# Moving the last transposes between two pairs of output tiles, and the final adds to GpSimd, in an attention and gated-MLP kernel

## The chip, the cores and the metric

The kernel runs on one core of one Trainium2 chip. The metric is the device time of one execution in microseconds (us). All runs quoted here are fast, with a mean granted TensorE clock of 0.999 or 1.0. The profile is of one execution, and its span is about 2 us shorter than that execution's device time. In the code, `ps_r` and `ps_acc` are tiles in PSUM, the memory that the matmuls write; the other tiles named here are in SBUF, the core's main on-chip memory. In the profile PE is TensorE, PEld its weight loads, DVE VectorE, ACT ScalarE, POOL GpSimd and SPq the DMA queue of SyncE. The differences of this case are below 0.1% of the time; so every experiment was timed in five rounds, beside runs of the kernel before on the same chip.

## The reference, cut to what matters

```python
xn = layernorm(x)                                   # x: 2048 x 512
q = (xn @ wq) split into 32 heads of 128            # k_cache, v_cache: 32 x 2048 x 128
p = softmax(q @ k_cache.T * 128**-0.5)
s = (p @ v_cache, heads side by side) @ wo          # 2048 x 512
g = silu(((relu(xn @ W_gate)) * (xn @ W_up)) @ W_down)
out = x + s * g
```

The output has 16 tiles of 128 rows, numbered 0 to 15. The product with `wo` is summed over groups of four heads. The first seven groups are already in `x_sb` (times `g`) when the last group is finished, so the "final add" of a tile is `x_sb += s_last * g`.

## The kernel before

TensorE is the limit of the whole kernel. Attention is a software pipeline: score matmuls, exponentials on ScalarE, probability-times-V matmuls. The final tiles 0 to 7 are produced inside that main loop. At its end the last block of 512 rows is normalised in two halves, and eight output tiles remain. Tiles 8 to 11 do not need the last block: they are the two "filler pairs" that keep TensorE busy while VectorE normalises it. Tiles 12 to 15 need it, transposed by TensorE and copied by ScalarE.

```python
def flush_last_transposes():
    s = ring_acquire()                        # one of three pairs of PSUM banks
    for k, (hh, Q, ob, bank, tok) in enumerate(pending_last):
        tp_ps = ps_r[:, 2 * s + k, :].bitcast(BF16)
        _wait(pe, tok)                        # VectorE has normalised this half
        # ... two pe.transpose of 128x128 from Onorm ...
        _wait(act, ptok)
        last_ot[bank] = sem_otc.sig(act.copy(OT_store[...], tp_ps[:, 0:256]))
    ring_tok[s] = list(last_ot.values())

def emit_final_tile(n, bank):
    # ... waits; four matmuls of 128x512 into ps_r[:, bank, 0:D] ...
    otok = sem_op.sig(ins)
    fb = fin_cnt[0] % NFT                     # NFT temporaries
    fin_cnt[0] += 1
    _wait(dve, otok)
    _wait(dve, fin_free[fb])
    mtok = sem_opa.sig(
        dve.tensor_tensor(fin_tmp[fb][:], ps_r[:, bank, 0:D], g_sb[:, n, :], ALU.mult))
    _wait(dve, mtok)
    if n == 0:
        _wait(dve, base_done[NT - 1])
    ftok = sem_opa.sig(
        dve.tensor_tensor(x_sb[:, n, :], x_sb[:, n, :], fin_tmp[fb][:], ALU.add))
    fin_free[fb] = ftok
    if Q == QB - 1 or j % 2 == 1:             # tiles 12 to 15: one store each
        n0 = n if Q == QB - 1 else n - 1
        _wait(sp, ftok)
        sem_out.sig(sp.dma_start(out_t[:, n0:n + 1, :], x_sb[:, n0:n + 1, :]))
    return mtok                               # frees the PSUM bank

# ... main loop ...
for n in range(NT - 8, NT - 4, 2):            # filler pairs (8, 9) and (10, 11)
    emit_M([(emit_final_tile, n), (emit_final_tile, n + 1)])
flush_last_transposes()
for n in range(NT - 4, NT, 2):                # (12, 13) and (14, 15)
    emit_M([(emit_final_tile, n), (emit_final_tile, n + 1)])
```

In the profile the multiply is line L767, the add L772, the output matmuls L759, the transposes L694, their copies L699, the half-tile normalisation L673 and L676, the store L777.

The softmax here doesn't subtract the row's maximum and nothing guards it: scores larger than these inputs give would overflow.

Of the kernel before, what the change touches and what calls it, by code (L numbers as in the profile page):

```python
# [5 lines left out]
BF16 = mybir.dt.bfloat16  # L6
F32 = mybir.dt.float32
ALU = mybir.AluOpType
# [21 lines left out]
def _wait(eng, tok):  # L30
    if tok is None:
        return
    sem, val = tok
    if val <= 0:
        return
    eng.wait_ge(sem.h, val)
# [15 lines left out]
def bass_recurrent_scan__mha_block_cached__glu_gated_reglu__prompt_kernel(  # L52
# [10 lines left out]
    out: bass.AP,  # L63
):
    _, S, D = A_x.shape
    _, H, Sk, Dh = A_k_cache.shape
    F = B_W_gate.shape[1]
    assert Dh == 128
# [4 lines left out]
    NT = S // 128  # L73
# [27 lines left out]
    dve = nc.vector  # L101
    sp = nc.sync
    pool = nc.gpsimd

    with ExitStack() as es:
        _cnt = [0]

        def S_(shape, dt, name):
            _cnt[0] += 1
            return es.enter_context(nc.sbuf_tensor(f"{name}_{_cnt[0]}", shape, dt))  # L110
# [4 lines left out]
        def newsem(unit=1):  # L115
            _cnt[0] += 1
            return _Sem(es.enter_context(nc.semaphore(f"sem{_cnt[0]}")), unit)
# [5 lines left out]
        x_sb = S_([128, NT, D], BF16, "x_sb")  # L123
# [53 lines left out]
        sem_xp = newsem()  # L177
# [5 lines left out]
        sem_opa = newsem()  # L183
# [14 lines left out]
        with nc.Block() as block:  # L198

            @block.tensor  # L200
            def _(_pe_eng):
# [91 lines left out]
                def wo_tok(g):  # L293
                    return (sem_wo[g % 2], 16 * (g // 2 + 1))
# [8 lines left out]
                def ring_acquire():  # L303
                    s = ring_cnt[0] % NSLOT
                    ring_cnt[0] += 1
                    _wait_all(pe, ring_tok[s])
                    ring_tok[s] = []
                    return s
# [222 lines left out]
                rz_sb = S_([128, 4, 1], F32, "rz_sb")  # L531
                Onorm = [S_([128, 4, Dh], BF16, "Onorm") for _ in range(NON)]
                OT_store = [S_([128, G, S], BF16, "OT_store") for _ in range(2)]
                fin_tmp = [S_([128, D], BF16, "fin_tmp") for _ in range(2)]

                qt_ready = {}
                qp_done_tok = {}
# [9 lines left out]
                def emit_M(items):  # L547
                    s = ring_acquire()
                    toks = [fn(*args, 2 * s + k) for k, (fn, *args) in enumerate(items)]
                    ring_tok[s] = toks  # L550
# [47 lines left out]
                base_done = {}  # L598
# [87 lines left out]
                def flush_last_transposes():  # L686
                    s = ring_acquire()
                    for k, (hh, Q, ob, bank, tok) in enumerate(pending_last):
                        tp_ps = ps_r[:, 2 * s + k, :].bitcast(BF16)
                        _wait(pe, tok)  # L690
                        ins = None
                        for jj in range(2):
                            j = 2 * bank + jj
                            ins = pe.transpose(tp_ps[:, jj * 128:(jj + 1) * 128], Onorm[ob][:, j, :], ident[:])  # L694
                        ptok = sem_ptr.sig(ins)
                        _wait(act, ptok)
                        c0 = Q * NQ + bank * 256
                        last_ot[bank] = sem_otc.sig(
                            act.copy(OT_store[(NG - 1) % 2][:, hh, c0:c0 + 256], tp_ps[:, 0:256])  # L699
                        )  # L700
                    ring_tok[s] = list(last_ot.values())
# [47 lines left out]
                def emit_final_tile(n, bank):  # L749
                    Q, j = divmod(n, 4)  # L750
                    if n == 0:
                        _wait(pe, wo_tok(gL))
                    if j == 0:
                        _wait(pe, (sem_tl[Q], sem_tl[Q].n))
                    if Q == QB - 1:
                        _wait(pe, last_ot[j // 2])
                    ins = None
                    for hh in range(G):
                        ins = pe.matmul(ps_r[:, bank, 0:D], OT_store[gL % 2][:, hh, n * 128:(n + 1) * 128],  # L759
                                        Wo_sb[gL % 2][:, hh, :], start=(hh == 0), stop=(hh == G - 1))  # L760
                    otok = sem_op.sig(ins)
                    fb = fin_cnt[0] % NFT
                    fin_cnt[0] += 1
                    _wait(dve, otok)
                    _wait(dve, fin_free[fb])
                    mtok = sem_opa.sig(
                        dve.tensor_tensor(fin_tmp[fb][:], ps_r[:, bank, 0:D], g_sb[:, n, :], ALU.mult))  # L767
                    _wait(dve, mtok)
                    if n == 0:
                        _wait(dve, base_done[NT - 1])  # L770
                    ftok = sem_opa.sig(
                        dve.tensor_tensor(x_sb[:, n, :], x_sb[:, n, :], fin_tmp[fb][:], ALU.add))  # L772
                    fin_free[fb] = ftok
                    if Q == QB - 1 or j % 2 == 1:
                        n0 = n if Q == QB - 1 else n - 1
                        _wait(sp, ftok)
                        sem_out.sig(sp.dma_start(out_t[:, n0:n + 1, :], x_sb[:, n0:n + 1, :]))  # L777
                    return mtok
# [16 lines left out]
                for Q in range(QB - 2):  # L795
                    for j in range(4):
                        plan.setdefault((LB + 2 + Q, 4 * (j // 2)), []).append((emit_final_tile, 4 * Q + j))
# [31 lines left out]
                assert not plan  # L829
                for n in range(NT - 8, NT - 4, 2):  # L830
                    emit_M([(emit_final_tile, n), (emit_final_tile, n + 1)])
                flush_last_transposes()
                for n in range(NT - 4, NT, 2):
                    emit_M([(emit_final_tile, n), (emit_final_tile, n + 1)])
                sp.wait_ge(sem_out.h, sem_out.n)
# [28 lines left out]
```

## Time and profile before

| | before |
|---|---|
| device time, median (six runs in all) | 1288.03 us (1287.91 to 1288.51) |
| span of the profiled run | 1285.8 us |
| TensorE busy | 99% of the span |
| VectorE, ScalarE, GpSimd busy | 30%, 78%, 1% |
| VectorE, pair of multiply and add, start to start, in the tail | 1.06 us |
| TensorE, four matmuls of one output tile | 0.87 us (in the chain view eight take 1.73 us) |
| last store's issue to the end of the span | 2.0 us |

Busy shares of a 1286 us span say nothing about its last 12 us. This is part 4 of the page of the kernel before, the chain of work that ended last:

```profile
PE 99%; DVE 1%; issue 0%; DMA 0%; ACT 0%
```

TensorE carries 99% of the chain, and VectorE (DVE) only 1%, but that 1% is the tail. The next lines are from the timeline of the kernel before, VectorE alone, tail only. The columns are start (us), duration (us), engine, line, operation, output and inputs, count, and in brackets the idle time before it and what ended it.

```profile
1274.13 0.17 DVE L673 RECIPROCAL rz_sb<-ps_acc 128x2 f32<-128x2 f32 x1 [0.35 <-PE ps_acc L722]
...
1275.21 0.68 DVE L767 TENSOR_TENSOR fin_tmp<-ps_r,g_sb 128x512 bf16<-128x512 f32 x1
1275.93 0.42 DVE L772 TENSOR_TENSOR x_sb<-x_sb,fin_tmp 128x512 bf16<-128x512 bf16 x1
1276.27 0.68 DVE L767 TENSOR_TENSOR fin_tmp<-ps_r,g_sb 128x512 bf16<-128x512 f32 x1
...
1282.64 0.68 DVE L767 TENSOR_TENSOR fin_tmp<-ps_r,g_sb 128x512 bf16<-128x512 f32 x1
1283.36 0.43 DVE L772 TENSOR_TENSOR x_sb<-x_sb,fin_tmp 128x512 bf16<-128x512 bf16 x1
```

There are no brackets behind the multiplies: VectorE hardly idles (it is busy for 5.90 us of the 6.11 us from 1276.20 to 1282.31). Its pairs follow each other every 1.06 us (1275.21, 1276.27), while TensorE delivers a tile every 0.87 us. So VectorE falls behind and the tail is its time: eight pairs, ending at 1283.79. The same stretch of the timeline shows TensorE and the copies that it waits for; the last row, from the timeline of SyncE, is the last store:

```profile
1277.50 0.39 PE L694 MATMUL ps_r<-ident,Onorm 128*128 128x128 bf16 x4
1277.81 0.65 ACT L699 COPY OT_store<-ps_r 128x256 bf16<-128x256 bf16 x2 [5.76 <-PE ps_r L694]
...
1278.33 3.61 PE L759 MATMUL ps_r<-Wo_sb,OT_store 128*128 128x512 bf16 x16 [0.44 <-ACT OT_store L699]
...
1283.81 0.33 SPq L777 DMA_DIRECT2D out_dram<-x_sb  x1
```

TensorE idles 0.44 us for ScalarE's copies, and still ends at 1281.94, almost 2 us before VectorE.

### The profile page before, as it was taken

How to read it: one execution, taken by the hardware profiler on the slowest of the kernel's cores; microseconds unless marked ns; L12 is line 12 of the kernel's file. 1: busy time of each engine (PE TensorE's matmuls, PEld its weight loads, DVE VectorE, ACT ScalarE, POOL GpSimd, SP SyncE). 2: the span in 40 equal slices, each digit the busy share in tenths (PEclk: the TensorE clock that was granted, in tenths of full speed). 3: DMA queues.
4: the chain of work that ended last, by engine and by line, in shares of the span. 5: the costliest groups of instructions: out<-in, count | busy, mean ns of one | idle time of the engine just before them, and what ended most of it. 6: DMA issues, size and time to landing. Idle time of an engine off the chain costs nothing.

```text
span 1285.8 us, 26847 instructions
## 1 busy us (share of the span) xinstructions
PE 1279.2 (99%) x11995; PEld 834.8 (65%) x11995; DVE 380.0 (30%) x682; ACT 1001.4 (78%) x1109; POOL 10.0 (1%) x21
## 2 busy tenths in 40 slices
PE   9999999999999999999999999999999999999998
PEld 4444476666666666666666666666666666666665
DVE  6333311112222222222222222222222222234456
ACT  3322399998888888888888888888888888888884
POOL 2000000000000000000000000000000000000000
PEclk9999999999999999999999999999999999999999
DMA  9500123232222332232322322332223321233302
GB/s 266 111 1 1 21 36 67 57 54 40 36 51 50 71 54 50 54 71 51 54 46 37 60 47 53 55 67 55 54 51 71 55 34 38 50 67 55 50 14 74
DMA packets 238801, 71.60 MB, mean 56 GB/s; under 512 B 225632, under 2 KB 238688, under 8 KB 238688
## 3 DMA queue, kind: packets, MB, share of 16 engines
q1 hardware_dynamic: 238400, 69.63, 27.8%
q8 instruction: 96, 1.57, 0.5%
q10 hardware_dynamic: 288, 0.26, 0.1%
q14 instruction: 17, 0.14, 0.0%
HBM read 32.77 MB, written 2.10 MB: 27 GB/s over the span
## 4 chain that ended last, share of the span: by engine, by line
PE 99%; DVE 1%; issue 0%; DMA 0%; ACT 0%
PE ps_acc L722 36%; PE ps_r L625 34%; PE ps_r L558 9%; PE ps_r L579 8%; PE ps_acc L504 4%; PE ps_r L485 4%; PE ps_r L481 4%; PE ps_r L759 1%; DVE fin_tmp L767 0%; PE ps_r L407 0%; DMA x_sb<-in_A_x_dram 0%; DVE stats L315 0%; ACT xnT L359 0%; PE ps_acc L353 0%; DVE x_sb L772 0%
## 5 line engine op out<-in xcount | busy, mean ns | idle before, releaser
L635 ACT ACTIVATE PT<-ps_r 128x1024 bf16<-128x1024 f32 x1024 | 952.5, 1054 | 167.7 <-PE ps_r L625 167.7
L722 PEld LDWEIGHTS ps_acc<-V_sb,PT 128*128 128x128 bf16 x8192 | 621.1, 98 | 241.7 <-ACT PT L635 3.5
L722 PE MATMUL ps_acc<-V_sb,PT 128*128 128x129 bf16 x8192 | 776.5, 220 | 0.0
L625 PE MATMUL ps_r<-QT_sb,KT_sb 128*128 128x512 bf16 x2048 | 754.1, 379 | 0.0
L652 DVE RECIPROCAL rz_sb<-ps_acc 128x4 f32<-128x4 f32 x127 | 23.3, 183 | 729.6 <-PE ps_acc L722 729.6
L625 PEld LDWEIGHTS ps_r<-QT_sb,KT_sb 128*128 128x128 bf16 x2048 | 195.0, 98 | 1.1 <-DVE QT_sb L569 0.4
L558 PE MATMUL ps_r<-xnT,Wq_sb 128*128 128x512 bf16 x512 | 130.9, 379 | 0.0
L579 PE MATMUL ps_r<-Wo_sb,OT_store 128*128 128x512 bf16 x448 | 114.6, 379 | 0.0
L569 DVE CAST QT_sb<-ps_r 128x512 bf16<-128x512 f32 x128 | 88.5, 692 | 48.1 <-PE ps_r L558 48.1
L558 PEld LDWEIGHTS ps_r<-xnT,Wq_sb 128*128 128x128 bf16 x512 | 49.9, 97 | 60.7 <-ACT PT L635 27.1
L655 DVE TENSOR_TENSOR Onorm<-ps_acc,rz_sb 128x512 bf16<-128x512 f32 x127 | 87.8, 691 | 4.4
L579 PEld LDWEIGHTS ps_r<-Wo_sb,OT_store 128*128 128x128 bf16 x448 | 43.8, 98 | 52.9 <-ACT PT L635 0.2
L448 ACT ACTIVATE gr_sb<-ps_r 128x512 bf16<-128x512 f32 x56 | 33.3, 596 | 51.5 <-PE ps_r L481 49.9
L592 DVE TENSOR_TENSOR s_acc<-s_acc,ps_r 128x512 f32<-128x512 f32 x96 | 66.0, 687 | 17.3 <-PE ps_r L579 17.3
L485 PE MATMUL ps_r<-xnT,Wu_sb 128*128 128x512 bf16 x212 | 54.4, 379 | 0.0
L481 PE MATMUL ps_r<-xnT,Wg_sb 128*128 128x512 bf16 x212 | 54.4, 379 | 0.0
L454 DVE TENSOR_TENSOR hT<-gr_sb,ps_r 128x512 bf16<-128x512 bf16 x56 | 38.4, 686 | 46.3 <-PE ps_r L485 42.0
L504 PE MATMUL ps_acc<-Wd_sb,hT 128*128 128x512 bf16 x224 | 49.0, 379 | 0.0
L510 ACT ACTIVATE sig_sb<-ps_acc 128x512 f32<-128x512 f32 x16 | 9.6, 597 | 38.8 <-PE ps_acc L504 38.8
L504 PEld LDWEIGHTS ps_acc<-Wd_sb,hT 128*128 128x128 bf16 x224 | 21.9, 98 | 26.4
L485 PEld LDWEIGHTS ps_r<-xnT,Wu_sb 128*128 128x128 bf16 x212 | 20.7, 98 | 25.0
L481 PEld LDWEIGHTS ps_r<-xnT,Wg_sb 128*128 128x128 bf16 x212 | 20.8, 98 | 24.8
(42 smaller groups left out, 138.7 us busy)
## 6 DMA issues: line engine op xcount, KB each, us to landing
V_sb<-in_A_v_cache_dram SPq DMA_DIRECT2D x32, 512.0 KB, 4.5
Wq_sb<-in_A_wq_dram SPq DMA_DIRECT2D x32, 128.0 KB, 2.4
Wo_sb<-in_A_wo_dram SPq DMA_DIRECT2D x8, 512.0 KB, 3.9
OT_store<-Onorm SPq DMA_TRANSPOSE x127, 2.4
Wd_sb<-in_B_W_down_dram SPq DMA_DIRECT2D x1, 1792.0 KB, 13.6
x_sb<-in_A_x_dram SPq DMA_DIRECT2D x3, 512.0 KB, 10.1
out_dram<-x_sb SPq DMA_DIRECT2D x6, 256.0 KB, 2.2
Wg_sb<-in_B_W_gate_dram SPq DMA_DIRECT2D x1, 768.0 KB, 9.8
```

Of the source, the lines that this page charges most:

```text
L454: dve.tensor_tensor(hT[par][:, fc, :], gr_sb[gk][:], ps_r[:, gb + 1, :], ALU.mult)
L481: ins = pe.matmul(ps_r[:, gb, :], Wg_sb[:, c, fs], xnT[:, c, qs], start=(c == 0), stop=(c == DC - 1))
L485: ins = pe.matmul(ps_r[:, gb + 1, :], Wu_sb[:, c, fs], xnT[:, c, qs], start=(c == 0), stop=(c == DC - 1))
L504: ins = pe.matmul(ps_acc[:, jb, 0:D], hT[par][:, fc, j * 128:(j + 1) * 128], Wd_sb[:, fc, :], start=(fc == 0), stop=(fc == FC - 1))
L558: ins = pe.matmul(ps_r[:, bank, :], Wq_sb[b][:, c, :], xnT[:, c, qs], start=(c == 0), stop=(c == DC - 1))
L569: etok = sem_qpe.sig(dve.tensor_copy(QT_sb[b][:, qs], ps_r[:, bank, :]))
L579: ins = pe.matmul(ps_r[:, bank, 0:D], OT_store[g % 2][:, hh, n * 128:(n + 1) * 128], Wo_sb[g % 2][:, hh, :], start=(hh == 0), stop=(hh == ...
L592: dve.tensor_tensor(s_acc[:, n, :], s_acc[:, n, :], ps_r[:, bank, 0:D], ALU.add)
L625: ins = pe.matmul(ps_r[:, 2 * s + tt, :], KT_sb[h % 2][:, t * 128:(t + 1) * 128], QT_sb[h % 2][:, qs], start=True, stop=True)
L635: act.activation(PT[pb][:], ps_r[:, 2 * s:2 * s + 2, :], ACTF.Exp, scale=scale)
L655: dve.tensor_tensor(Onorm[ob][:], o_ap, rz_sb[:].to_broadcast([128, 4, Dh]), ALU.mult))
L722: ins = pe.matmul(o_ap, PT[pb][:, tt, j * 128:(j + 1) * 128], V_sb[vb][:, t, 0:VW], start=(t == 0 and j % 2 == 0), stop=(t == KT - 1 and j ...
```

## The change

The intent is to hide TensorE's wait for the copies behind tiles 10 and 11, and to take the adds off VectorE, which lags in the tail. GpSimd is idle there. The last tile's add stays on VectorE. There are four temporaries in place of two, so that multiplies don't wait for GpSimd. This is the whole diff; unchanged lines are mostly left out:

```diff
-                fin_tmp = [S_([128, D], BF16, "fin_tmp") for _ in range(2)]
+                fin_tmp = [S_([128, D], BF16, "fin_tmp") for _ in range(4)]
@@ emit_final_tile
-                    _wait(dve, mtok)
+                    eng, sem = (dve, sem_opa) if n == NT - 1 else (pool, sem_xp)
+                    _wait(eng, mtok)
                     if n == 0:
-                        _wait(dve, base_done[NT - 1])
-                    ftok = sem_opa.sig(
-                        dve.tensor_tensor(x_sb[:, n, :], x_sb[:, n, :], fin_tmp[fb][:], ALU.add))
+                        _wait(eng, base_done[NT - 1])
+                    ftok = sem.sig(
+                        eng.tensor_tensor(x_sb[:, n, :], x_sb[:, n, :], fin_tmp[fb][:], ALU.add))
@@ end
                 for n in range(NT - 8, NT - 4, 2):
                     emit_M([(emit_final_tile, n), (emit_final_tile, n + 1)])
-                flush_last_transposes()
+                    if n == NT - 8:
+                        flush_last_transposes()
```

## The prediction

> **What bounds the kernel now.** The page gives TensorE 99% busy of a 1285.8 us span at full clock, and the chain of waits is 99% TensorE. The change touches only the last ~12 us, where the chain is different. There it leaves TensorE at 1274.1 us (end of the last probability-times-V matmuls) and runs on VectorE to the end: after the last two normalisations come eight pairs of a multiply (128x512 out of PSUM, 0.68 us) and an add (128x512 bf16, 0.43 us). Starts of multiplies in the timeline: 1275.21, 1276.27, ... 1282.64, a pair every 1.06 us. TensorE needs only about 0.865 us per output tile (16 matmuls in 3.6 us) and ends at 1281.9 us, so VectorE is the limit of the tail by then: last add ends at 1283.79 us, the last store takes the remaining 2.0 us.
>
> **What the change does.**
> 1. Transposes after the first filler pair: TensorE waited 0.6 us in all (waits view: 0.59 us of weight load, 0.44 us of matmul, overlapping) for ScalarE's two copies of 0.32 us. Now tiles 10 and 11 (1.7 us of matmuls) hide them. The norm results are ready at 1275.3, before TensorE reaches the transposes (about 1275.8). TensorE ends about 0.4 us earlier, at 1281.5. This was not on the critical chain, since VectorE lagged.
> 2. VectorE loses seven of the eight tail adds. Alone it would follow TensorE: last multiply about 1281.6 to 1282.3, last add to 1282.75, 1.0 us earlier than before.
> 3. GpSimd takes seven adds in the tail (tiles 8 to 14), on two SBUF inputs. No such add is in the trace. A one-input GpSimd pass over 128x512 bf16 starts every 0.75 us here. The Trainium skill, "GPSIMD Engine Reference", section "Performance versus the Vector engine", states about 1.8 cycles per element [...] (768 ns for 512, which this trace shows: 768 ns mean) and about 2.6 for a two-input add. My estimate from both: 2.6/1.8 x 0.768 = 1.11 us, with dispatch 1.1 to 1.2. That is slower than VectorE's whole pair (1.06 us). First add starts at about 1276.0; seven take 7.8 to 8.4 us and end at 1283.8 to 1284.4.
> 4. The last add stays on VectorE with two SBUF inputs. The skill, "SBUF — State Buffer", has VectorE and GpSimd exclude each other on a shared port pair in that case, so it waits for a GpSimd add rather than running at 1282.3: it ends at about 1284.3 to 1284.8. No run shows this yet. The last two stores then also follow each other closely.
> 5. Adds of tiles 0 to 7 move too, inside the main loop, where neither engine is the limit: nothing. Four temporaries suffice; multiplies wait little.
>
> **Sum.** Final add about 0.5 to 1.0 us later than 1283.79, then the same 2.0 us: the tail's limit moves from VectorE to GpSimd and the time gets slightly worse, by about 0.7 us of 1288.09, far under 2%.
>
> Predicted: 1288.8 us, range 1287.4 to 1289.8. Chances: faster by over 2% 0.005, within 2% 0.99, slower 0.005.
>
> **What would show it.** Timeline of the tail: GpSimd adds back to back, start to start about 1.1 us, ending after 1283.5 (right) or keeping up with TensorE's 0.865 us (wrong; then about 1 us is gained, to 1287.1). TensorE's last matmul near 1281.5 with no wait for ScalarE's copies. The last VectorE add waiting or lengthened while GpSimd adds run. Last stores' end to start gap unchanged at 2 us.
>
> **What would make it wrong.** GpSimd's bf16 add at under 1.0 us each; no mutual blocking of the last add (0.4 us less); VectorE's multiplies slowed by GpSimd's SBUF reads (they have one SBUF input, so I expect none); longer semaphore latency from GpSimd to the store queue; run-to-run spread of 0.5 us.

## The result, and the profile after

| | before | after |
|---|---|---|
| device time, median of six runs | 1288.03 us (1287.91 to 1288.51) | 1288.64 us (1288.43 to 1288.95) |
| ratio, fast runs | | 1.0004, 95% interval 0.9992 to 1.0017 |
| span of the profiled run | 1285.8 us | 1286.7 us |

The ratio is the mean time of one kernel's fast runs over that of the other's of the same rounds, so it is not quite the ratio of the medians. The spans differ by more than the medians, because the profiled execution of the kernel before took 1287.7 us, less than any of its six timed runs. By the interval the two are the same. The six runs of each do not come as close as that sounds: all but one of those after lie above all of those before. The experiments below repeat it (1288.77 against 1287.99).

The chain of work that ended last, page of the changed kernel:

```profile
PE 98%; POOL 1%; DVE 0%; DMA 0%; POOLq 0%; ACT 0%; issue 0%; DVEq 0%
```

GpSimd (POOL) has taken the place of VectorE in the tail. The timeline of the changed kernel, VectorE alone:

```profile
1274.34 0.17 DVE L673 RECIPROCAL rz_sb<-ps_acc 128x2 f32<-128x2 f32 x1 [1.01 <-PE ps_acc L722]
...
1279.85 0.69 DVE L767 TENSOR_TENSOR fin_tmp<-ps_r,g_sb 128x512 bf16<-128x512 f32 x1 [0.17 <-PE ps_r L759]
1280.72 0.69 DVE L767 TENSOR_TENSOR fin_tmp<-ps_r,g_sb 128x512 bf16<-128x512 f32 x1 [0.17 <-PE ps_r L759]
1281.58 0.69 DVE L767 TENSOR_TENSOR fin_tmp<-ps_r,g_sb 128x512 bf16<-128x512 f32 x1 [0.17 <-PE ps_r L759]
1282.31 0.86 DVE L773 TENSOR_TENSOR x_sb<-x_sb,fin_tmp 128x512 bf16<-128x512 bf16 x1
```

From the third on, VectorE now waits for TensorE before each multiply (the brackets), so it keeps up; its last multiply starts 1.06 us earlier. TensorE no longer waits for the copies (no brackets in the first row below), and its last matmul ends at 1281.54. The last add took 0.86 us where such adds took 0.43. TensorE, GpSimd and the stores of the changed kernel, from timelines of each engine and short windows:

```profile
1276.20 5.34 PE L759 MATMUL ps_r<-Wo_sb,OT_store 128*128 128x512 bf16 x24
...
1276.18 8.00 POOL L773 TENSOR_TENSOR x_sb<-x_sb,fin_tmp 128x512 bf16<-128x512 bf16 x7 [1.38 <-DVE fin_tmp L767]
...
1277.29 2.27 POOL L773 TENSOR_TENSOR x_sb<-x_sb,fin_tmp 128x512 bf16<-128x512 bf16 x2
1278.40 2.27 POOL L773 TENSOR_TENSOR x_sb<-x_sb,fin_tmp 128x512 bf16<-128x512 bf16 x2
...
1281.73 2.44 POOL L773 TENSOR_TENSOR x_sb<-x_sb,fin_tmp 128x512 bf16<-128x512 bf16 x2
...
1284.20 0.33 SPq L778 DMA_DIRECT2D out_dram<-x_sb  x1
1284.58 0.43 SPq L778 DMA_DIRECT2D out_dram<-x_sb  x1
```

The seven adds of tiles 8 to 14 are one merged row of 8.00 us with no idle time between them. Windows of about one add show the starts: 1276.18, 1277.29, 1278.40, every 1.11 us. The last pair (1281.73) took 2.44 us in place of 2.27. Then come two stores: tile 14's at 1284.20, and tile 15's at 1284.58, though its add was done at 1283.17. The two are in one queue, in program order.

The tail starts at slightly different moments in different profiles, because of the 1274 us before it. So from here on, tail times are counted from the start of the first half-tile reciprocal (1274.13 before, 1274.34 after), and are differences of the timeline's numbers:

| | before | after |
|---|---|---|
| last multiply starts | 8.51 | 7.24 |
| last add of any engine ends | 9.66 (VectorE, tile 15) | 9.83 (GpSimd, tile 14) |
| last store is issued | 9.68 | 10.24 |
| span ends | 11.7 | 12.4 |

Of the roughly 0.6 us lost (0.7 us between these two profiles), 0.17 us is the later last add, about 0.4 us is tile 15's store waiting behind tile 14's, and 0.1 us is the longer issue of that store (0.43 us against 0.33).

### The profile page after: what moved, and what is told of

It reads as the page before. It is cut to its first block, busy times and chain, and to the rows that moved or that the text cites. A ratio compares the mean times of both kernels' runs of the same rounds, so it can differ in the third digit from the quotient of the medians.

```text
span 1286.7 us, 26845 instructions
## 1 busy us (share of the span) xinstructions
PE 1279.4 (99%) x11995; PEld 834.8 (65%) x11995; DVE 375.1 (29%) x667; ACT 1001.3 (78%) x1109; POOL 27.0 (2%) x36
## 4 chain that ended last, share of the span: by engine, by line
PE 98%; POOL 1%; DVE 0%; DMA 0%; POOLq 0%; ACT 0%; issue 0%; DVEq 0%
PE ps_acc L722 36%; PE ps_r L625 34%; PE ps_r L558 9%; PE ps_r L579 8%; PE ps_acc L504 4%; PE ps_r L485 4%; PE ps_r L481 4%; PE ps_r L759 1%; POOL x_sb L773 1%; PE ps_r L407 0%; DMA x_sb<-in_A_x_dram 0%; DVE stats L315 0%; POOLq L198 0%; ACT xnT L359 0%; PE ps_acc L353 0%
## 5 line engine op out<-in xcount | busy, mean ns | idle before, releaser
L773 POOL TENSOR_TENSOR x_sb<-x_sb,fin_tmp 128x512 bf16<-128x512 bf16 x15 | 17.0, 1166 | 1231.0 <-DVE fin_tmp L767 1231.0
```

## The experiments

Theory: in the tail, seven GpSimd adds at 1.11 us each replace VectorE's pairs at 1.06 us as the limit; moving the transposes gains nothing by itself; the issue order of the last stores costs the rest. Rivals: the order of the transposes matters, the hop to another engine costs something in the main loop, or it is the blocked last VectorE add that sets the end. All runs were correct. The kernel before measured 1288.02, 1287.95 and 1287.99 us (medians of nine runs) in the three sets of rounds.

### 1. The order alone

The kernel before with only the move of `flush_last_transposes()`.

> Only the transposes move; all final adds stay on VectorE and two temporaries stay. Theory (VectorE's multiply-add pairs at 1.06 us limit the old tail, TensorE's wait for ScalarE's copies was hidden): TensorE's last matmul ends about 0.4 us earlier (near 1281.5), the starts of VectorE's multiplies do not move, time equal to the kernel before within 0.1 us. Rival (the wait for the copies was on the critical path): about 0.4 to 0.6 us faster than before.

Measured: 1288.03 us (1287.89 to 1288.31) against 1288.02. TensorE's wait for the copies is gone. The VectorE pairs are untouched: the last add ends 9.65 us into the tail, against 9.66. The wait was off the critical path, and hiding it gains nothing while VectorE lags. The rival falls.

### 2. The adds alone

The changed kernel with the transposes back in their old place.

> Only the adds move to GpSimd; the transposes stay after the second filler pair. Theory (seven GpSimd adds at 1.11 us start to start set the tail): the adds run back to back from about 1276.2 as in the changed kernel, the time is that of the changed kernel, 1288.6, within 0.15 us. Rival (TensorE's order matters to the changed kernel's end): TensorE's later end, by 0.4 us, shows in the time, 1289.0.

Measured: 1288.55 us (1288.44 to 1288.76), 0.53 above before, and not 1289.0. So nearly all of the loss comes with the adds on GpSimd. There is a detail that was not expected. VectorE, a little later in this version, and GpSimd, timelines:

```profile
1283.25 1.36 DVE L773 TENSOR_TENSOR x_sb<-x_sb,fin_tmp 128x512 bf16<-128x512 bf16 x1
...
1276.52 7.81 POOL L773 TENSOR_TENSOR x_sb<-x_sb,fin_tmp 128x512 bf16<-128x512 bf16 x7 [1.37 <-DVE fin_tmp L767]
1283.18 1.15 POOL L773 TENSOR_TENSOR x_sb<-x_sb,fin_tmp 128x512 bf16<-128x512 bf16 x1
```

Here GpSimd's last add had started 0.07 us before VectorE's became ready. VectorE's add took 1.36 us and ended at 1284.61, 0.28 us after GpSimd's end (1283.18 + 1.15 = 1284.33); GpSimd was not held up (7.81 us against 8.00 in the changed kernel). In the changed kernel VectorE's add was ready during GpSimd's last add but one, got in between the two, and pushed the last one back.

### 3. Tile 15's store first

```diff
+                held_store = []
@@ emit_final_tile
+                        if n == NT - 2:              # tile 14: store later
+                            held_store.append((n, ftok))
+                            return mtok
                         _wait(sp, ftok)
                         sem_out.sig(sp.dma_start(out_t[:, n0:n + 1, :], x_sb[:, n0:n + 1, :]))
+                        if n == NT - 1:
+                            m, htok = held_store.pop()
+                            _wait(sp, htok)
+                            sem_out.sig(sp.dma_start(out_t[:, m:m + 1, :], x_sb[:, m:m + 1, :]))
```

> The changed kernel, but tile 15's store is issued before tile 14's. In the changed kernel tile 15's add ends at 1283.17 and its store waits until 1284.68, behind the store of tile 14, whose GpSimd add ends at 1284.17. Theory (the issue order of the two stores costs one issue slot after the last GpSimd add, about 0.47 us): the last store is issued at about 1284.2, the time falls by 0.4 to 0.5 us, to about 1288.15. Rival (the end is a fixed 2.5 us after the last GpSimd add, whatever the order): no change from 1288.6.

(The 1284.68 in that text was misread; a narrower window of the timeline shows 1284.58. The slot between the two starts is 0.38 us, and the second issue itself takes 0.10 us longer, 0.43 against 0.33.)

Measured: 1288.08 us (1288.07 to 1288.22), 0.06 above before. The store queue of this version, last two stores of the timeline:

```profile
1283.23 0.43 SPq L782 DMA_DIRECT2D out_dram<-x_sb  x1
...
1284.13 0.33 SPq L786 DMA_DIRECT2D out_dram<-x_sb  x1
```

Tile 15's store goes out at 1283.23, while GpSimd is still adding tile 14, and nothing is left in line at the end. Almost the whole loss is gone without making any add faster. By the trace the last store still goes out 9.87 us into the tail, against 9.68 before, because GpSimd's last add is as late as in the changed kernel; so small a rest the times don't resolve. The Trainium skill, "Perfetto Trace Analysis", section "DMA Instruction — HWDGE (DVE, Sync)", says that the issuing sequencer is free for its next instruction only after a DMA's descriptors are generated. This trace agrees: one issue occupies the queue for 0.33 to 0.43 us.

### 4. The last product left in PSUM, twice

```diff
+                    prod = ps_r[:, bank, 0:D] if n == NT - 1 else fin_tmp[fb][:]
-                        dve.tensor_tensor(fin_tmp[fb][:], ps_r[:, bank, 0:D], g_sb[:, n, :], ALU.mult))
+                        dve.tensor_tensor(prod, ps_r[:, bank, 0:D], g_sb[:, n, :], ALU.mult))
-                        eng.tensor_tensor(x_sb[:, n, :], x_sb[:, n, :], fin_tmp[fb][:], ALU.add))
+                        eng.tensor_tensor(x_sb[:, n, :], x_sb[:, n, :], prod, ALU.add))
```

VectorE's last add then reads one tile of SBUF and one of PSUM.

> The changed kernel, but the last product stays in PSUM, so VectorE's last add has one SBUF input in place of two. Theory (two SBUF inputs on VectorE and a GpSimd add exclude each other, which stretched VectorE's add from 0.43 to 0.86 us and the last GpSimd add from 1.15 to 1.34 us): VectorE's add takes about 0.69 us without a wait, the last GpSimd add 1.15 us, time about 0.19 us less than the changed kernel, 1288.45. Rival (both were stretched by something else, such as the stores): the GpSimd add stays at about 1.34 us, time 1288.6.

Measured: 1288.49 us (1288.42 to 1288.75), too close to 1288.64 of other rounds to tell by time. It was repeated beside the unedited changed kernel:

> The changed kernel unedited, in the same rounds as the next run, so that small differences are compared on one chip: about 0.6 us above before, 1288.6.

> The version with the last product in PSUM again, beside the changed kernel. Theory (mutual exclusion lengthened the last GpSimd add by 0.19 us and the end with it): 0.1 to 0.2 us below the changed kernel of the same rounds. Rival: no difference.

Measured in the same rounds: the changed kernel 1288.77 us (1288.53 to 1288.83), this version 1288.55 us (1288.39 to 1288.66). The means differ by 0.16 us, and the ranges overlap. The trace is clearer; timelines of the first of the two runs:

```profile
1282.43 0.69 DVE L774 TENSOR_TENSOR x_sb<-x_sb,ps_r 128x512 bf16<-128x512 bf16 x1
...
1282.95 1.15 POOL L774 TENSOR_TENSOR x_sb<-x_sb,fin_tmp 128x512 bf16<-128x512 bf16 x1
```

VectorE's add took 0.69 us, the ordinary time of a pass that reads PSUM in this kernel, and ran during GpSimd adds that keep their 1.15 us. With two SBUF inputs the same two instructions took 0.86 and 1.34 us. The Trainium skill, "SBUF — State Buffer", section "SBUF: two separate sides", describes this as an exclusive lock on a port pair shared by the two engines, held for a whole instruction by the one that starts first. Runs 2 and 4 and the changed kernel agree with it: 1.36 us with GpSimd first, 0.86 us in between, 0.69 us with no need of the pair. The two repeated runs show the same again (0.85 and 0.69 us).

These traces also show what GpSimd's slower rate costs by itself. Where no VectorE add got in between (runs 2 and 4), its seven adds end 9.65 and 9.66 us into the tail, when VectorE's eight pairs ended before (9.66). So the whole 0.17 us of the later last add is the add of VectorE that got in between.

### 5. All final adds on GpSimd

```diff
-                    eng, sem = (dve, sem_opa) if n == NT - 1 else (pool, sem_xp)
+                    eng, sem = (pool, sem_xp)
```

> The changed kernel with the last tile's add on GpSimd too: eight tail adds there, none on VectorE. Theory (GpSimd's adds follow each other every 1.11 us and set the end): the last ends at about 1276.2 + 7 x 1.11 + 1.15 = 1285.1 in the changed kernel's time, 0.95 us later than its last GpSimd add, and its store is issued at once in place of second in line (0.47 us); sum +0.45 us, 1289.1. Rival (GpSimd is not the limit, the last VectorE add's wait is): equal to or below 1288.6.

Measured: 1289.11 us (1288.85 to 1289.17) against 1287.95. The timeline of GpSimd:

```profile
1276.24 8.92 POOL L773 TENSOR_TENSOR x_sb<-x_sb,fin_tmp 128x512 bf16<-128x512 bf16 x8 [1.37 <-DVE fin_tmp L767]
```

The eighth add ends 10.77 us into the tail (first reciprocal at 1274.39), 1.11 us after seven unblocked ones. An eighth add makes the tail longer at GpSimd's pace, as the theory had it; the limit is GpSimd's rate, not the blocking of VectorE's last add.

### 6. GpSimd in the main loop alone

```diff
-                    eng, sem = (dve, sem_opa) if n == NT - 1 else (pool, sem_xp)
+                    eng, sem = (dve, sem_opa) if n >= NT - 8 else (pool, sem_xp)
```

> GpSimd adds only tiles 0 to 7, inside the main loop; the eight tail tiles are added by VectorE; the transposes are moved. Theory (in the main loop neither engine is the limit): equal to the kernel before and to the order alone, 1288.0 within 0.15 us. Rival (the hop to GpSimd costs in the main loop, by delaying multiplies, stores or normalisations): part or all of the changed kernel's 0.6 us appears here.

Measured: 1287.98 us (1287.93 to 1288.07) against 1287.95. The slower adds of tiles 0 to 7 cost nothing: in the main loop GpSimd idles 3.0 us between pairs of adds. The loss is made in the tail alone. One such pair in the timeline:

```profile
1267.43 2.27 POOL L773 TENSOR_TENSOR x_sb<-x_sb,fin_tmp 128x512 bf16<-128x512 bf16 x2 [3.00 <-DVE fin_tmp L767]
```

### 7. Sharing the adds by what each engine can finish

GpSimd keeps the tail tiles 8 to 12; VectorE adds tiles 13, 14 and 15 after its last multiply; tile 14's store goes out on ScalarE's queue.

```diff
-                    eng, sem = (dve, sem_opa) if n == NT - 1 else (pool, sem_xp)
-                    # ... add and store of tile n ...
+                    late.append((n, fb, mtok))       # late = [] is set once, above the function
+                    if NT - 3 <= n < NT - 1:
+                        return mtok
+                    for m, mb, mt in late:
+                        eng, sem = (dve, sem_opa) if m >= NT - 3 else (pool, sem_xp)
+                        # ... add of tile m from fin_tmp[mb], as before ...
+                            q = act if m == NT - 2 else sp
+                            _wait(q, ftok)
+                            sem_out.sig(q.dma_start(out_t[:, n0:m + 1, :], x_sb[:, n0:m + 1, :]))
+                    late.clear()
```

> GpSimd keeps the adds up to tile 12; VectorE adds tiles 13 to 15 after its last multiply, and tile 14's store goes out on ScalarE's queue so that the three last stores don't queue behind each other. Theory: five GpSimd adds end at 5.6 us after the first, before VectorE's last multiply ends, so nothing is blocked: VectorE's three adds take 0.43 us or less each, the last ends 9.1 us after the start of the first half-tile reciprocal (9.66 before, 9.83 in the changed kernel for its last GpSimd add); time 0.4 to 0.6 us below before, about 1287.5. Rival (the tail has a fixed end set by the stores or by TensorE): 1288.0.

Measured: 1287.36 us (1287.11 to 1287.39) against 1287.95 (1287.80 to 1288.32). Timelines of VectorE and GpSimd:

```profile
1282.28 1.09 DVE L778 TENSOR_TENSOR x_sb<-x_sb,fin_tmp 128x512 bf16<-128x512 bf16 x3
...
1276.27 5.60 POOL L778 TENSOR_TENSOR x_sb<-x_sb,fin_tmp 128x512 bf16<-128x512 bf16 x5 [1.37 <-DVE fin_tmp L768]
```

GpSimd's five adds end at 1281.87, before VectorE starts its three, which take 1.09 us together with nothing blocked. The last add ends 8.94 us into the tail (first reciprocal at 1274.43).

To tell the adds from the extra queue, the same version was run with all stores on SyncE's queue:

> The sharing version again, but all its stores on SyncE's queue, so that the adds and the extra queue are told apart. Theory (stores of one queue are issued one after the other, about 0.37 to 0.47 us each): tiles 13, 14 and 15 are ready 0.33 us apart, so the last store is issued about 0.2 to 0.4 us late; time 1287.55 to 1287.75, against 1287.36 with the extra queue and 1288.0 before. Rival (the queue does not matter here): 1287.36.

Measured: 1287.62 us (1287.32 to 1287.79) against 1287.99. The last store of this version:

```profile
1283.64 0.45 SPq L785 DMA_DIRECT2D out_dram<-x_sb  x1
```

It is issued 9.15 us into the tail (first reciprocal at 1274.49), in place of 8.96. The sharing of the adds gives about 0.37 us over the kernel before, and the second queue the other 0.2 us; the two versions were timed in different rounds and on different chips, and their ranges overlap slightly. No run defers the adds of tiles 13 to 15 with all adds on VectorE, so how much of the 0.37 us needs GpSimd at all is open.

### 8. No GpSimd: ScalarE copies out of PSUM

The kernel before with the transposes moved, and ScalarE, idle in the tail, copying tiles 8 to 14 as bf16, so that VectorE multiplies from SBUF:

```diff
+        sem_cp = newsem()
+                fin_cp = [S_([128, D], BF16, "fin_cp") for _ in range(8)]
@@ emit_final_tile
+                    free_tok = None
+                    src = ps_r[:, bank, 0:D]
+                    if NT - 8 <= n < NT - 1:
+                        _wait(act, otok)
+                        otok = free_tok = sem_cp.sig(act.copy(fin_cp[n % 8][:], src))
+                        src = fin_cp[n % 8][:]
                     _wait(dve, otok)
                     _wait(dve, fin_free[fb])
-                        dve.tensor_tensor(fin_tmp[fb][:], ps_r[:, bank, 0:D], g_sb[:, n, :], ALU.mult))
+                        dve.tensor_tensor(fin_tmp[fb][:], src, g_sb[:, n, :], ALU.mult))
-                    return mtok
+                    return free_tok or mtok
```

> No GpSimd at the end at all: the transposes move, and idle ScalarE copies tiles 8 to 14 out of PSUM as bf16, so that VectorE's multiply reads two bf16 SBUF tiles (about 0.43 us, as its bf16 add, in place of 0.69). Theory (VectorE's pair at 1.06 us against TensorE's 0.865 is what limited the old tail): the pairs take about 0.7 us, VectorE keeps TensorE's pace, the last add ends 8.9 us after the first half-tile reciprocal's start (9.66 before); time 0.6 to 0.9 us below before, about 1287.3. Rival (no gain beyond moving the limit elsewhere): 1288.0.

Measured: 1287.39 us (1287.26 to 1287.51) against 1287.95. Timeline, tile 12 and the last tile:

```profile
1279.04 0.59 ACT L770 CAST fin_cp<-ps_r 128x512 bf16<-128x512 f32 x1 [0.28 <-PE ps_r L761]
...
1279.65 0.43 DVE L775 TENSOR_TENSOR fin_tmp<-fin_cp,g_sb 128x512 bf16<-128x512 bf16 x1
1280.12 0.42 DVE L780 TENSOR_TENSOR x_sb<-x_sb,fin_tmp 128x512 bf16<-128x512 bf16 x1
...
1282.90 0.43 DVE L780 TENSOR_TENSOR x_sb<-x_sb,fin_tmp 128x512 bf16<-128x512 bf16 x1
```

With bf16 from SBUF the multiply takes 0.43 us in place of 0.68, and VectorE keeps TensorE's pace. The last add ends 8.95 us into the tail (first reciprocal at 1274.38), as in the sharing version. Both versions beat the kernel before by about 0.6 us of 1288: their slowest run is below the fastest of its nine runs. By ratio it is 0.9995 in both, with intervals (0.9982 to 1.0007, and 0.9983 to 1.0008) that include 1.

## Why the prediction was right

The time, 1288.64 us, lies 0.16 us from the predicted 1288.8 and within the range, and "within 2%" held. Point by point:

- The limit of the old tail was VectorE's pairs and not TensorE's wait for the copies. Right: the order alone gave 1288.03 against 1288.02.
- TensorE ends near 1281.5 with no wait. Right: 1281.54.
- VectorE alone would finish its last multiply at about 1282.3. Right: 1281.58 + 0.69 = 1282.27.
- GpSimd's add at 1.1 to 1.2 us, hence a new and slightly slower limit. Right: 1.11 us start to start, seven adds from 1276.18 to 1284.17; predicted 1276.0 to 1283.8 or 1284.4. The eighth add and the shared version confirm that this rate is the limit. But the rate alone did not make the tail longer: seven unblocked adds end where VectorE's eight pairs had ended (9.65 and 9.66 us into the tail, against 9.66).
- The main loop's adds are free. Right: 1287.98 against 1287.95.
- The last VectorE add and GpSimd exclude each other. The mechanism was right, but the placing was wrong. The prediction had this add end "at about 1284.3 to 1284.8", after all of GpSimd's. It got in before GpSimd's last add and ended at 1283.17; what it cost was 0.19 us on GpSimd's last add.
- "Final add about 0.5 to 1.0 us later than 1283.79, then the same 2.0 us." This sum was right only because two terms were mis-sized in opposite directions. In the tail's own time the final add came 0.17 us later, not 0.5 to 1.0. The last store, which the prediction gave no cost of its own (it said only that the last two stores "follow each other closely"), started 0.41 us after it, because the finished tile 15 stood in line behind tile 14, and from its issue to the end of the span it took 2.1 us and not 2.0. Putting tile 15's store first took the loss from 0.6 to 0.06 us.

What stays open: whether the transposes' new place costs 0.1 to 0.2 us in the changed kernel, by letting VectorE's last add in before GpSimd's. The trace of run 2, with the transposes in their old place, suggests it (GpSimd's seven adds take 7.81 us there and 8.00 in the changed kernel, and the last store is issued 10.05 us into the tail and not 10.24), but the times of run 2 and of the changed kernel come from different rounds and overlap. No run joins 3 and 4, which should leave no loss if the account above is whole.

## What to carry to other kernels

Before you move work from a lagging engine to an idle one, compare the idle engine's time for the piece with the pace that must be kept: here 1.11 us on GpSimd against 0.87 us from TensorE and 1.06 us for both of VectorE's instructions, so only the part that GpSimd finished in time (five of eight tiles, the one split that was tried) was worth moving. In a tail, look at what the last store waits for, because a finished tile behind an unfinished one in an in-order queue costs an issue slot. A wait on the engine that limits the whole kernel can still be free where another engine is behind it.

## What the Trainium skill lacked or had wrong

- "GPSIMD Engine Reference", section "Performance versus the Vector engine": its figure of about 2.6 cycles per element for a two-input add was right here: 512 elements at 1.2 GHz make an estimate of 1.11 us, and the runs show 1.11 us start to start. But it comes with fp32 measurements alone, and its ratio of about 2 to VectorE, measured in fp32, does not carry over to bf16: the same 128x512 bf16 add took 0.43 us on VectorE and 1.15 us on GpSimd, about 2.7 times as long. Back to back, VectorE did three in 1.09 us, about the time from one GpSimd start to the next.
- "SBUF — State Buffer", section "SBUF: two separate sides": the exclusive lock is described, but not what happens to a VectorE instruction that waits while GpSimd instructions follow each other without a gap. Here it did not wait for all of them: it ran between two (0.86 us instead of 0.43), and the GpSimd add after it took 1.34 us instead of 1.15.
- "Perfetto Trace Analysis", section "DMA Instruction — HWDGE (DVE, Sync)": this section describes the occupied sequencer without a duration. Stores of 128 KB took 0.33 us to issue, and 0.43 to 0.45 us right behind another.
